# Buffers, feature sums and engine choices in a fused attention and gated-layer block on one core

## The chip, the cores and the metric

The kernel runs on one core of one Trainium2 chip. A core has five engines that work side by side and meet through semaphores: TensorE (PE in the profile, with its weight loads shown as PEld), VectorE (DVE), ScalarE (ACT), GpSimd (POOL) and SyncE (SP), which here only issues transfers. Matrix products land in PSUM, eight banks of 512 float32 numbers for each of 128 partitions; everything else lies in SBUF. The metric is device time in microseconds (us) of one execution, lower is better. The kernel before took 207.77 us (median of three runs, 207.37 to 208.1).

## The reference

The input x has 2048 rows of 448 bf16 numbers. Two blocks follow each other, each with a layer norm ahead of it and an addition of its own input behind it:

```python
def _A_ref(x, wqkv, w_phi, wo):                      # H = 16 heads, Dh = 28
    q, k, v = ...                                    # x @ wqkv, split by head
    pq = einsum("bhsd,hdf->bhsf", q, w_phi); pk = einsum("bhsd,hdf->bhsf", k, w_phi)
    phi_q = concat([softmax(pq), softmax(-pq)])      # over the 28 features of a head
    phi_k = concat([softmax(pk), softmax(-pk)])
    kv = einsum("bhsf,bhsd->bhfd", phi_k, v); z = einsum("bhsf->bhf", phi_k)
    num = einsum("bhqf,bhfd->bhqd", phi_q, kv)
    den = einsum("bhqf,bhf->bhq", phi_q, z)[..., None] + 1e-6
    return (num / den).reshape(B, S, D) @ wo

def _B_ref(x, w_gate, w_up, w_down):                 # F = 1792
    return (sigmoid(x @ w_gate) * (x @ w_up)) @ w_down

h  = x + _A_ref(layernorm(x), ...)
h2 = h + _B_ref(layernorm(h), ...)
```

So it is linear attention: a feature map of keys and values is summed over all rows (kv and z) before any query can be answered, and then a gated layer follows. The sum over all rows is the one place where everything has to come together.

## The kernel before

The 2048 rows are 16 tiles of 128 (t = 0 to 15); most later work goes by pairs of tiles (pr = 0 to 7), the queries by blocks of four tiles (c = 0 to 3), the gated layer by chunks of 2, 4, 4, 4 and 2 tiles.

Work is written as named tasks, each with the engines that may do it, the tasks it depends on and, for a PE task, the PSUM banks it may use. The order of all tasks is not computed at run time: the table `ORDER` (lines 40 to 88) lists one number for each task, 32 × (number of the task) + 4 × (choice of bank) + (choice of engine). `stored` reads it, and `emit` gives each engine its tasks in that order as a fixed instruction list, with a semaphore wait ahead of a task wherever something it needs is made by another engine. So each engine works strictly in order: if the task at the head of its list has to wait, all behind it wait.

The stages, by the names of the tasks:

- Loads. x comes in six transfers (x0 to x12 by first tile), the weights of attention in others, all ahead of the weights of the gated layer. `wqT`, `xT`, `oT` and `hT` are transposes done by transfers from SP's queue.
- First norm (lines 577 to 606). For each tile `bst` (statistics) and `agg` on VectorE; by batches of 1, 1, 2, 4, 4, 4 tiles `ve` and `rstd` (the power −0.5, on GpSimd), and for the later batches `mm` and `nm`, which make the negative mean times that power. `xn` writes the normalised tile to `xn_pad`, a ring of `NXP` tiles; tiles 0 to 3 are transposed on PE (`xP`, `xT`), the others by transfers.
- Keys and values (lines 626 to 700). `pa` and `pb` are the two parts of a tile's products with the folded key weights and the value weights, in two banks. `ekp` and `ekm` are the exponentials of both signs on ScalarE (`ek`, a ring of `NEK`), `v1` copies the values out. Then the softmax: `sa` and `ss` make the sums over the 28 features, `rs` the reciprocals, `phi` scales the exponentials (a ring of `NPHI`), and `kv` adds the tile's product of features and values in bank 4.
- In `sa` the two halves of the 28 features are added, 448 numbers from 896; `ss` then sums the rest with a reduce. A tile takes this way if it is in `SPLIT`, which holds all 16 tiles. `sa` writes `half_s`, a ring of `NSA` = 2.
- Queries (`qa`, `q`, `eqp`, `eqm`, lines 727 to 748), then `kvz`, which takes the summed features out of bank 4 once the last `kv` is done.
- Attention output (lines 758 to 895): `num` (products with `kvz`), `ocp` (copy to SBUF, ScalarE or VectorE), `rSm`, `rr`, `b`, `c`, `rd`, `o` on VectorE (the normalising factors and the output), `oT`, `woa` and `wo_` (product with wo), `h` or `hc` (addition of x), the second norm (`bst2`, `agg2`, `ve2`, `rstd2`, `hn`) and `hT`. Pair 0 is transposed on PE (`oP`, `hP`), the other pairs by transfers.
- Gated layer (lines 917 to 979): `ga` and `gu` are the two parts of gate and up for 128 of the 1792 columns, `sig` on ScalarE, `hh` on VectorE, `dn` the product with w_down, `fin` the last addition and `st` the store. It needs all its weights and the transposed tiles of its chunk.

In the order before, the scalings `phi` are all on VectorE; four of the sixteen `sa` are on VectorE (tiles 6, 10, 12, 15), twelve on GpSimd; `xn` of tiles 0 to 5, 8, 13, 14 on VectorE, the seven others on ScalarE; of the copies `ocp` tiles 1 and 3 on VectorE. The first products of features, `kv` of tiles 1 to 3, stand in PE's list ahead of the second part of tile 7, the one of tile 0 behind tile 2.

Of the kernel before, what the change touches and what calls it, by code (L numbers as in the profile page):

```python
# [5 lines left out]
dt = mybir.dt  # L6
# [34 lines left out]
544 576 0 480 1152 609 224 737 128 28416 160 640 96 28448 352 801 192 28480 768 256 448 28512 384 896 28544  # L41
992 28576 1952 832 28608 28640 960 1984 2017 2112 28672 2048 673 28704 2144 705 2080 28736 2336 2176 928 28768
2208 2272 864 1184 1088 2368 2304 1316 2240 1216 2720 1120 1384 1344 1260 288 2656 1409 4144 2400 1588 512
1281 4160 2432 1440 1636 2592 1600 4072 9632 1472 2464 1520 28800 2496 1665 28832 4096 4204 1537 2528 4276
4225 1056 2624 4576 2688 2560 4289 2752 2785 3104 2848 2816 4608 3168 10272 3040 4516 5824 1024 2881 5536 2913
4712 2945 5568 3136 3200 3072 4320 2976 4544 3232 5632 4736 3264 5792 3008 5664 5888 4640 5696 6304 4352 5601
320 4672 6368 3297 5728 6336 5856 1760 5920 3328 1700 6080 1832 3616 5760 1793 3744 3360 4772 6048 3392 6112
3425 3680 6144 1888 3456 4800 5952 1856 3776 3648 4384 6400 3552 4832 1728 6176 6560 4904 5984 6592 10304 3488
4864 6208 6656 10176 6432 4928 6624 10208 3712 3584 6464 6848 4964 3809 6240 6816 6496 3520 6016 6272 3873
6881 6912 6528 7072 4416 4992 7136 6688 3840 7104 5024 6944 7392 10240 6720 5096 1921 6976 9664 3904 7360 6752  # L50
5056 9696 7328 7169 5120 3936 7008 10408 7616 3969 7584 7200 7424 4448 6784 7840 7040 7232 7648 10432 7680
7456 7904 5216 7488 7872 7264 10464 5160 7520 4032 7712 7936 5248 5184 7744 10496 9728 7776 7296 7552 4001
8096 7808 8161 4480 8128 5284 7968 8384 8352 5352 8193 10336 8416 8448 8224 5312 10144 8000 5376 8256 416 8608
8032 10532 8640 8672 8705 8864 8064 8480 10560 8896 8288 8928 5476 9792 10592 8736 8960 9760 5416 8512 8544
10624 5504 8768 5440 8992 9376 8800 10788 9408 9152 9024 9473 9120 8320 8576 9056 9184 8832 10816 9440 9504
9216 10656 9536 10848 9248 11048 9568 10880 9280 10688 9312 9088 10720 9344 9824 9600 9856 11072 11424 10752
10368 11524 12524 11104 11553 11456 11488 12545 12452 12480 13216 11584 13292 11616 11136 11648 10916 12576
13312 11680 11176 12608 12640 9888 13248 14060 10944 11712 12672 14080 11200 11744 10976 12704 11904 13344
11864 12736 11804 11232 13376 12768 11873 12800 11808 11008 13408 11936 13440 11264 13996 14756 13472 11968
13504 14016 11304 13536 12032 13568 12096 14112 14828 14784 12064 11328 12128 14144 12160 12000 14176 12836  # L60
12192 14848 12224 14208 15584 12864 12288 15616 12256 12408 12896 12348 13600 12353 14240 12416 12928 15524
13632 15552 14272 17836 13664 11360 17856 18084 14880 17888 17952 12992 11392 18112 17920 17984 13696 18476
9920 18144 18016 13024 18600 12960 14304 13728 13056 14336 18048 18496 13088 18176 18624 13760 18528 18208
18656 18560 18340 18688 18240 13792 13152 16364 9952 18272 18728 13825 13120 16384 18368 18304 13856 13184
18752 14912 18400 18976 13920 18784 16300 18432 19008 13888 14372 18816 19040 13952 14944 16320 17064 14400
19072 14976 9984 19232 14432 18860 17088 19264 18880 16416 19492 18912 19368 18944 19520 15008 16448 19392
19552 20076 19424 19584 15648 20196 15040 15072 19456 15104 20096 14464 19944 15680 20128 10016 19296 20224
19328 10048 20160 19968 20256 20448 20000 20032 20588 20288 15144 16480 17124 15712 15168 10080 17152 20608
15200 10112 20480 20640 20708 20672 20512 15744 19112 19820 15232 16512 20736 20544 19136 15776 20768 19840
16544 19168 21344 19200 15808 20328 19872 20800 19904 21220 14528 20352 15296 20844 15264 16576 20384 14496  # L70
15328 20416 21248 15360 15392 14560 20864 21280 15840 15456 21480 15872 20896 21312 20928 21376 14593 20964
14624 21408 21100 14656 21440 20992 16608 15424 16640 17184 21120 21024 17216 14688 15904 17248 21152 15488
21056 21504 15936 14720 21536 19620 19712 19648 21184 21568 15968 21996 19744 22248 22496 22016 22528 22048
# [10 lines left out]
27200 25472 27552 26816 27584 28012 25504 26336 25536 27240 28032 26368 28064 27748 26400 27264 26432 27776  # L84
28096 27296 26848 27328 27372 26880 27808 27880 26912 27840 27392 26944 27620 27904 27424 27648 64 27456 26144
27680 27936 25964 26240 25984 26016 26048 26272 27968 26304 27712 26176 28136 26080 26112 19680 21952 23936
28224 24032 28160 21856 26208 28320 19776 28256 24128 28288 28192 28352 28384
"""


# [938 lines left out]
```

## Time and profile before

| | us |
|---|---|
| median of three runs | 207.77 |
| the profiled execution | 207.67 |
| its span, first to last instruction | 205.9 |
| PE busy | 197.2 |
| VectorE busy | 135.6 |
| ScalarE busy | 96.5 |
| GpSimd busy | 30.6 |

The page and its views name engines, lines and operations. A group reads: line, engine, operation, output and inputs, shapes, number of instructions, then busy time in us and mean length of one in ns, then the idle time of the engine ahead of them and what ended it. A stretch of the table of stretches has its two ends, its length, and for each engine the time it was busy in it. A timeline gives start, length and number of instructions of each piece. The chain that ended last is followed back from the last instruction, each step to what released it. [...]

The span is not the time of an execution: 1.8 us lie around it.

### The profile page before, as it was taken

What the parts mean: (1) busy time and instruction counts of PE and PEld (TensorE: products, weight loads), DVE (VectorE), ACT (ScalarE), POOL (GpSimd) and SP (SyncE); (2) the same over time, 40 slices, a digit from 0 to 9 for tenths busy, and PEclk for the clock granted to TensorE, in tenths of its full rate; (3) what the DMA queues carried; (4) which work ended last, traced back from release to release, by engine and by line L of the source; (5) the groups of instructions that cost most, each with busy time, mean ns of one, the idle gap of its engine ahead of it and who ended that gap; (6) DMA issues with size and microseconds to landing.
All of it is one profiled execution on the core that took longest, in us unless ns stands there. A gap on an engine that the chain in (4) does not pass through costs nothing.

```text
span 205.9 us, 5431 instructions
## 1 busy us (share of the span) xinstructions
PE 197.2 (96%) x2278; PEld 107.1 (52%) x2278; DVE 135.6 (66%) x312; ACT 96.5 (47%) x172; POOL 30.6 (15%) x56
## 2 busy tenths in 40 slices
PE   7899998998988999999999999999999999999993
PEld 2544555455445876554444444544444455796553
DVE  2999999997998996789823875435446415351241
ACT  2579999799998773443311333003334400442000
POOL 3738653420003110001100001100001000000000
PEclk9999999999999999999999999999999999999999
DMA  5996477764022493700450000620000031000034
GB/s 167 279 277 128 76 188 200 181 223 142 3 57 48 73 173 81 197 3 3 94 111 3 0 0 3 124 51 0 3 0 5 2 79 20 0 3 0 25 111 156
DMA packets 35109, 16.94 MB, mean 82 GB/s; under 512 B 26828, under 2 KB 34060, under 8 KB 35084
## 3 DMA queue, kind: packets, MB, share of 16 engines
q1 hardware_dynamic: 34140, 15.78, 33.1%
q10 hardware_dynamic: 944, 0.80, 1.4%
q8 instruction: 18, 0.29, 0.6%
q14 instruction: 7, 0.06, 0.1%
HBM read 8.98 MB, written 1.84 MB: 53 GB/s over the span
## 4 chain that ended last, share of the span: by engine, by line
PE 78%; DVE 12%; ACT 4%; DMA 2%; issue 1%; POOL 1%
PE bank L934 42%; PE bank L968 21%; PE bank L637 5%; PE bank L833 4%; PE bank L736 3%; DMA x_sb<-in_A_x_dram 2%; DVE phi L684 2%; PE bank L696 1%; DVE ssum L673 1%; DVE xn_pad L603 1%; DVE st L583 1%; ACT xn_pad L602 1%; ACT ek L659 1%; DVE b_sb L792 1%; DVE b_sb L795 1%
## 5 line engine op out<-in xcount | busy, mean ns | idle before, releaser
L934 PE MATMUL bank<-xnT,wg_sb 64*128 64x512 bf16 (+1 forms) x490 | 87.4, 333 | 0.1
L934 PE MATMUL bank<-xnT,wu_sb 64*128 64x512 bf16 (+1 forms) x490 | 87.4, 333 | 0.0
L943 ACT ACTIVATE sg_sb<-bank 128x512 f32<-128x512 f32 (+1 forms) x70 | 34.6, 513 | 77.9 <-PE bank L934 74.0
L951 DVE SCALAR_TENSOR_TENSOR hh<-sg_sb,bank 128x512 bf16<-128x512 f32 (+1 forms) x70 | 39.1, 576 | 28.4 <-ACT sg_sb L943 28.1
L934 PEld LDWEIGHTS bank<-xnT,wg_sb 64*128 64x128 bf16 x490 | 45.3, 94 | 21.9 <-issue 1.9
L934 PEld LDWEIGHTS bank<-xnT,wu_sb 64*128 64x128 bf16 x490 | 45.1, 94 | 15.5
L968 PE MATMUL bank<-wd_sb,hh 128*128 128x448 bf16 (+1 forms) x238 | 43.1, 342 | 0.0
L968 PEld LDWEIGHTS bank<-wd_sb,hh 128*128 128x128 bf16 x238 | 22.9, 98 | 20.1 <-issue 1.4
L975 DVE SCALAR_TENSOR_TENSOR x_sb<-bank,x_sb 128x448 bf16<-128x448 f32 (+1 forms) x17 | 9.9, 594 | 28.3 <-PE bank L968 28.3
L637 PE MATMUL bank<-Wk,xnT 64*128 64x448 bf16 x112 | 22.1, 350 | 0.4 <-ACT Wq L425 0.3
L637 PE MATMUL bank<-Wv,xnT 64*128 64x448 bf16 x112 | 21.6, 350 | 0.0
L746 ACT ACTIVATE eq<-bank 128x1024 bf16<-128x1024 f32 x16 | 16.3, 1067 | 0.7 <-PE bank L736 0.6
L871 POOL TENSOR_SCALAR rs<-mv 128x2 f32<-128x2 f32 x5 | 1.3, 256 | 99.6 <-DVE mv L869 50.3
L667 POOL TENSOR_TENSOR half_s<-ek 128x448 f32<-128x448 bf16 x12 | 12.9, 1078 | 15.3 <-ACT ek L657 7.0
L425 ACT CAST opm<-bank 128x960 bf16<-128x960 f32 x14 | 13.7, 1014 | 2.8 <-PE bank L772 2.1
L833 PE MATMUL bank<-wo_sb,oT 64*128 64x448 bf16 x112 | 13.3, 350 | 0.9 <-DVE oT L425 0.6
L736 PE MATMUL bank<-xnT,Wq 64*128 64x512 bf16 x112 | 14.0, 377 | 0.1
L637 PEld LDWEIGHTS bank<-Wk,xnT 64*128 64x128 bf16 x112 | 9.1, 94 | 6.9 <-PE bank L637 1.0
L637 PEld LDWEIGHTS bank<-Wv,xnT 64*128 64x128 bf16 x112 | 9.2, 94 | 4.3
L684 DVE TENSOR_TENSOR phi<-ek,rsum 128x896 bf16<-128x896 bf16 x16 | 10.3, 655 | 0.3 <-PE bank L696 0.2
L583 DVE BATCH_NORM_STATS2 st<-x_sb 128x6 f32<-128x448 bf16 x16 | 9.4, 612 | 1.7 <-DMA x_sb<-in_A_x_dram 1.7
L657 ACT ACTIVATE ek<-bank 128x448 bf16<-128x448 f32 x16 | 9.7, 630 | 1.3 <-PE bank L637 1.3
(91 smaller groups left out, 185.4 us busy)
## 6 DMA issues: line engine op xcount, KB each, us to landing
wg_sb<-in_B_w_gate_dram SPq DMA_DIRECT2D x4, 448.0 KB, 3.8
wu_sb<-in_B_w_up_dram SPq DMA_DIRECT2D x4, 448.0 KB, 3.7
out_dram<-x_sb SPq DMA_DIRECT2D x15, 112.0 KB, 1.8
wd_sb<-in_B_w_down_dram SPq DMA_DIRECT2D x7, 224.0 KB, 2.7
x_sb<-in_A_x_dram SPq DMA_DIRECT2D x2, 448.0 KB, 5.8
wq_raw<-in_A_wqkv_dram SPq DMA_DIRECT2D x4, 128.0 KB, 5.3
x_sb<-in_A_x_dram SPq DMA_DIRECT2D x2, 224.0 KB, 4.5
x_sb<-in_A_x_dram ACTq DMA_DIRECT2D x2, 224.0 KB, 4.9
```

The lines of the kernel that those rows point to most:

```text
L425: return e.copy(dst, src) if hasattr(e, "activation") else e.tensor_copy(dst, src)
L583: task(("bst", t), "dve", dve(D), lambda e, t=t: e.bn_stats(st1[:, t % 4, :], X(t)), [x_ld[t], opt(("agg", t - 4))])
L637: r = e.matmul(bank[bk][:, 0:D], lhsT=half(xnT, hi)[:, t, k, :], rhs=half(w, hi)[:, k, :], start=(i == 0), stop=(i == 6), tile_position=(6 ...
L667: task(("sa", t), None, 0.88, lambda e, t=t, s=s: e.tensor_tensor(half_s[:, t % NSA].rearrange("p (a n) -> p a n", a=4 * G), ek[:, s].rear ...
L684: task(("phi", t), None, 1.68, lambda e, t=t, s=s: e.tensor_tensor(phi[:, t % NPHI, :, :, 0:DH, :].rearrange("p a g d h -> p (a g) d h"), ...
L736: r = e.matmul(bank[bb[j]], lhsT=half(Wq2, hi)[:, k, 2 * g:2 * g + 2].rearrange("p c d h -> p (c d h)"), rhs=half(xnT, hi)[:, 4 * c:4 * c ...
L746: task((key, gp, c), "act", act_p(1024), lambda e, gp=gp, c=c, sg=sg, nm=nm: e.activation(eq[c][:, sg, 2 * gp:2 * gp + 2, :], wide[got(nm) ...
L833: r = e.matmul(bank[bb[j]][:, 0:D], lhsT=half(oT, hi)[:, pr % NO, j, k, :], rhs=half(wo_sb, hi)[:, k, :], start=(i == 0 and not res), stop ...
L934: r = e.matmul(bank[b][:, 0:N], lhsT=half(w, hi)[:, k, fs], rhs=half(hnT, hi)[:, t0:t0 + n, k, :], start=(i == 0), stop=(i == 6), tile_pos ...
L943: task(("sig", f_, c), "act", act_p(N), lambda e, j=j, N=N, nm=nm: e.activation(sg_sb[:, j % NSG, 0:N], bank[got(nm)[0]][:, 0:N], ACT.Tanh ...
L951: task(("hh", f_, c), "dve", dve(N), lambda e, j=j, N=N, nm=nm, f_=f_, c=c: e.scalar_tensor_tensor(hhT[c % 2][:, f_, 0:N], sg_sb[:, j % NS ...
L968: r = e.matmul(bank[b][:, c0:c1], lhsT=hhT[c % 2][:, f_, o:o + P], rhs=wd_sb[:, f_, c0:c1], start=(f_ == 0), stop=(f_ == FT - 1))
```

## The change

Five things are edited:

- Rings: `xn_pad` 8 to 10 tiles, `ek` 4 to 6, `phi` 3 to 6, `v1` 4 to 6, `opm` (the copied output products) 3 to 4.
- `SPLIT` is empty, so there is no `sa`, and `ss` of every tile is one reduce on VectorE over 896 numbers.
- `xn` of tiles 4 to 15 may also be done on GpSimd. (The test that picks the form of the instruction now asks for the task's engine.)
- `o` also waits for the two copies of pair 0's transposed output, which use the same ring.
- `ORDER` is another table, with other choices of engine and bank.

Decoded, the new table differs most in these places. `phi` of tiles 0, 1, 5, 7, 9, 10, 11 and 13 is on GpSimd. `xn` of tiles 5 to 11, 14 and 15 is on GpSimd, of 4 and 12 on ScalarE, of 13 and 0 to 3 on VectorE. Of the copies `v1`, tiles 0, 5 and 10 move from VectorE to ScalarE, 12 and 14 the other way. `ocp` of tile 7 moves to VectorE, one of pair 0's transposed copies from VectorE to ScalarE, and one the other way for the second norm. Of the variance steps `ve2`, five move from GpSimd to VectorE, one the other way. In PE's list the first value products stand ahead of the first key products, and `kv` of tiles 0, 1 and 2 stand together ahead of the second part of tile 7; `kv` of tiles 10 to 15 stand together behind the four query blocks that go ahead of them. On SP's queue the load of tiles 8 to 11 moves behind all loads of query and value weights, and the last two loads of the gate and up weights behind `oT` of pair 1.

```diff
@@ -38,53 +38,52 @@
 ORDER = """
-544 576 0 480 1152 609 224 737 128 28416 160 640 96 28448 352 801 192 28480 768 256 448 28512 384 896 28544
...
+544 737 0 480 1152 609 352 576 27904 128 288 640 27936 769 512 448 27968 800 224 256 28000 320 960 384 160 32
...
@@ -336,8 +335,8 @@
-    NXP, NEK, NPHI, NV, NOP, NO, NHP, NSG, NSA = 8, 4, 3, 4, 3, 2, 2, 4, 2
-    SPLIT = range(NT)
+    NXP, NEK, NPHI, NV, NOP, NO, NHP, NSG, NSA = 10, 6, 6, 6, 4, 2, 2, 4, 2
+    SPLIT = ()
@@ -386,7 +385,7 @@
-        half_s = sb("half_s", [P, NSA, D], dt.float32)
+        half_s = sb("half_s", [P, NSA, D], dt.float32) if len(SPLIT) else None
@@ -598,11 +597,11 @@
                     dst, src = xn_pad[:, s, :].rearrange("p (a n) -> p a n", a=2), lap(X(t))
-                    if hasattr(e, "activation"):
+                    if K.tasks[("xn", t)].eng == "act":
                         return e.activation(dst, src, ACT.Identity, bias=nm1[:, t:t + 1], scale=rs1[:, t:t + 1])
                     return e.tensor_scalar(dst, src, mv1[:, t, 0:1], rs1[:, t:t + 1], op0=ALU.subtract, op1=ALU.mult)
                 task(("xn", t), None, dve(160), f, [("rstd", a), opt(("nm", a)), free],
-                     engs=("dve",) if a < 4 else ("act", "dve"))
+                     engs=("dve",) if a < 4 else ("act", "dve", "pool"))
@@ -799,7 +798,7 @@
-                fac(rden[:, s2], DH), ALU.mult), [("rd", pr), opt(("oT", pr - NO))])
+                fac(rden[:, s2], DH), ALU.mult), [("rd", pr), opt(("oT", pr - NO)), opt(("oT", pr - NO, 0)), opt(("oT", pr - NO, 1))])
```

91 rows, old and new, of the table ORDER are left out of this document.

## The prediction

> **What bounds the kernel now.** I read four views in this order: the busy times of the page, the table of stretches, the chain that ended last, and then the groups and timelines of the stretch that the first three point at. The page's first part and the stretches (columns of a stretch: length, then busy time and instruction count of PE, PEld, DVE, ACT, POOL, then clock and DMA):
>
> ```profile
> PE 197.2 (96%) x2278; PEld 107.1 (52%) x2278; DVE 135.6 (66%) x312; ACT 96.5 (47%) x172; POOL 30.6 (15%) x56
> ```
> ```profile
> 4.40:16.00 11.60, 10.55 (x99) 5.68 (x97) 11.33 (x35) 7.32 (x16) 5.96 (x12) 1.00 1.17 272
> 16.00:49.40 33.40, 32.49 (x528) 16.95 (x528) 31.37 (x71) 31.38 (x60) 15.19 (x18) 1.00 0.68 175
> 49.40:67.10 17.70, 15.22 (x304) 8.19 (x304) 16.40 (x39) 16.81 (x22) 1.62 (x2) 1.00 0.16 31
> 67.10:202.70 135.60, 135.59 (x1344) 75.03 (x1344) 75.69 (x166) 39.73 (x77) 5.82 (x11) 1.00 0.22 48
> ```
>
> PE is busy 96% of the span, but the last row says where it can and cannot be helped: from 67.1 to 202.7 us it is idle 0.01 us, so nothing there can be gained. What the change can win lies ahead of 67 us, where PE, DVE and ACT are all nearly full. The chain tells which of them leads:
>
> ```profile
> 16.08 0.70 ACT xn_pad L602
> ...
> 18.08 0.42 ACT v L425
> 18.50 0.44 ACT ek L659
> ...
> 31.57 1.87 DVE phi L684 x2
> ...
> 47.76 0.88 PE bank L696 x48
> 48.64 0.75 PE bank L736 x6
> ...
> 62.01 0.52 POOL rs L871
> ...
> 62.61 1.11 POOL rs L873
> ...
> 63.75 0.42 DVE hn_pad L877
> ...
> 66.61 0.46 PE bank L934 x7
> ```
>
> Three stages: up to 48.64 us the keys' features (normalise, project, exponentials, sums, scaling, and their products on PE); up to 66.61 the attention output and the second norm of the first tiles; then the gated layer, PE alone. I call the end of the last feature product, 48.64 us, T. VectorE sets it. Its timeline holds the first sum, pairs that show the pace, the stalls and the last scaling:
>
> ```profile
> 7.79 1.03 DVE L603 TENSOR_SCALAR xn_pad<-x_sb,mv,rs 128x512 bf16<-128x512 bf16 x1
> ...
> 16.03 0.62 DVE L673 TENSOR_REDUCE ssum<-half_s 128x32 f32<-128x448 f32 x1
> ...
> 23.67 1.15 DVE L684 TENSOR_TENSOR phi<-ek,rsum 128x896 bf16<-128x896 bf16 x2
> ...
> 25.74 1.14 DVE L673 TENSOR_REDUCE ssum<-half_s 128x32 f32<-128x448 f32 x2
> ...
> 28.81 1.06 DVE L603 TENSOR_SCALAR xn_pad<-x_sb,mv,rs 128x512 bf16<-128x512 bf16 x1
> ...
> 31.57 1.87 DVE L684 TENSOR_TENSOR phi<-ek,rsum 128x896 bf16<-128x896 bf16 x2
> ...
> 47.18 0.62 DVE L684 TENSOR_TENSOR phi<-ek,rsum 128x896 bf16<-128x896 bf16 x1
> ```
>
> Two sums of 0.61 take 1.14 and two scalings of 0.62 take 1.15: the next instruction starts some 0.08 before the last ends, so a price on the path is the duration less 0.08. From 16.03 to 47.80 are 31.8 us. The groups, shapes kept apart (busy, mean ns):
>
> ```profile
> L684 DVE TENSOR_TENSOR phi<-ek,rsum 128x896 bf16<-128x896 bf16 x16 | 10.3, 655 | 0.3 <-PE bank L696 0.2
> L673 DVE TENSOR_REDUCE ssum<-half_s 128x32 f32<-128x448 f32 x16 | 9.6, 603 | 0.0
> L873 POOL TENSOR_TENSOR rs<-rs,neghalf 128x2 f32<-128x2 f32 x8 | 6.2, 770 | 5.8 <-DVE rs L871 5.4
> L682 DVE RECIPROCAL rsum<-ssum 128x32 bf16<-128x32 f32 x16 | 5.3, 339 | 0.2
> L588 POOL TENSOR_TENSOR rs<-rs,neghalf 128x4 f32<-128x4 f32 x3 | 3.3, 1115 | 0.3 <-DVE rs L586 0.3
> L425 DVE CAST opm<-bank 128x960 bf16<-128x960 f32 x2 | 2.2, 1152 | 0.5 <-PE bank L772 0.5
> L443 POOL TENSOR_SCALAR_AFFINE_SELECT ident<-ident 128x128 bf16<-128x128 bf16 x1 | 0.3, 292 | 0.0
> L450 DVE TENSOR_REDUCE dmask<-ident 128x2 f32<-128x112 bf16 x1 | 0.3, 270 | 1.5 <-POOL ident L443 1.5
> L436 POOL TENSOR_SCALAR_AFFINE_SELECT maskW<-maskW 112x4 f32<-112x4 f32 x1 | 0.2, 195 | 0.1
> ```
>
> My sum for VectorE in those 31.8 us: 16 sums at 0.53 = 8.5; 16 scalings at 0.54 = 8.6; 16 reciprocals at 0.26 = 4.2; 4 half sums at 0.54 = 2.2; 3 copies of v at 0.54 = 1.6; 4 statistics at 0.53 = 2.1; 3 normalisations at 0.33 = 1.0; small ones 0.6. That is 28.8. The two slow rows (1.06 against the usual 0.41, 1.87 against 1.15) add 0.65 and 0.72, and 1.6 are waits and gaps. VectorE is the bound of the stage, and the stalls are GpSimd's doing:
>
> ```profile
> 7.28 1.08 POOL L524 TENSOR_TENSOR Wp<-wphd,maskW 112x224 bf16<-112x224 bf16 x2
> ...
> 19.89 1.90 POOL L667 TENSOR_TENSOR half_s<-ek 128x448 f32<-128x448 bf16 x2 [0.44 <-ACT ek L657]
> ...
> 28.49 1.23 POOL L667 TENSOR_TENSOR half_s<-ek 128x448 f32<-128x448 bf16 x1 [1.52 <-ACT ek L657]
> ...
> 31.79 1.16 POOL L667 TENSOR_TENSOR half_s<-ek 128x448 f32<-128x448 bf16 x1 [0.28 <-ACT ek L659]
> ```
>
> The normalisation begun at 28.81 ends at 29.87, just after GpSimd's half sum (29.72); the second scaling of 31.57 ends at 33.44, after 32.95 plus its own half microsecond; the normalisation of 7.79 sits through both products of GpSimd, which end at 8.36.
>
> **The change, part by part.** The new table, decoded number by number (task, bank, engine), gives the order on each engine.
>
> Feature sums in one instruction. The half sums go: 4 on VectorE, 12 on GpSimd. Each of the 16 sums reads 896 numbers instead of 448. From 112 elements in 270 ns (same pattern, bf16) to 448 in 603 ns is 0.99 ns an element, so 448 more cost 0.45: 0.98 each, 15.7 in all, +7.2 on VectorE. I bound it by 0.9 and 1.1 each, that is 1.3 below and 1.9 above.
>
> Scalings on GpSimd. Tiles 0, 1, 5, 7, 9, 10, 11, 13: 8 × 0.54 = 4.3 off VectorE. On GpSimd a two-input instruction of 448 runs at 0.95 (two in 1.90), so 896 at about 1.85. It lies beside VectorE, except where GpSimd holds VectorE up, below. [...]
>
> Normalisations on GpSimd. Tiles 5 to 11, 14 and 15 go to GpSimd, 4 and 12 to ScalarE (0.70 each on its path, seven before), so ScalarE loses 3.5 us, and VectorE keeps one of the last twelve. The price on GpSimd is not in the trace: the one-input rows (4 elements 195 ns, 128 in 292) give 0.78 ns an element, 0.59 for 512; the two-input row gives 1.06. I take 0.65, near the one-input rows, since it reads one tensor; both ends stay for the range.
>
> More buffers. The rings of ek, phi and v go to six, of padded tiles to ten. PE and ScalarE may run six tiles ahead of the scaling instead of four or three, so a late scaling stops PE only where its product stands in PE's queue. They take no time.
>
> Where the stage begins. VectorE now has its first eight statistics, four normalisations and a dozen small ones done at about 11.8 (4.46 + 4.2 + 1.3 + 1.2 + 0.6 of waits). Then 1.05 on GpSimd for the power −0.5 of four variances (row of 1115), 0.2 for the mean; ScalarE does tile 4 (0.70), two copies of v (0.42) and four exponentials (0.44): the first sum starts at 16.6, against 16.03. The load of tiles 8 to 11 moves from seventh to eleventh on SP's queue:
>
> ```profile
> 8.02 0.47 SPq L461 DMA_DIRECT2D wq_raw<-in_A_wqkv_dram  x1
> ```
> ```profile
> wu_sb<-in_B_w_up_dram SPq DMA_DIRECT2D x4, 448.0 KB, 3.7
> ...
> x_sb<-in_A_x_dram SPq DMA_DIRECT2D x2, 448.0 KB, 5.8
> ```
>
> The eleventh was issued at 8.02; with 5.8 to landing it is there at 13.8, VectorE wants it at 12.4, and the statistics behind it (3.6) have until 16.6. So it costs between nothing and 0.8; I take 0.2. In exchange the two loads of v's weights go ahead, which only helps.
>
> The sum to T. VectorE from 16.8: 15.7 + 4.3 + 4.2 + two v copies 1.1 + two statistics 1.1 + one normalisation 0.3 + small ones 0.8 = 27.5, the same 1.6 of waits, and the time GpSimd holds it. Walking GpSimd's queue: three normalisations 13.2 to 15.2, power and mean to 17.0, three more to 18.9, scalings 1 and 0 from 19.1 to 22.8, tile 10 to 23.5. VectorE comes to its first scaling (tile 2) at 23.1: 0.4 lost. Tile 4's meets tiles 15 and 14 (0.15), tile 14's meets 13 and 11 (0.3). Together 0.85, against the 1.4 of before. 16.8 + 27.5 + 1.6 + 0.85 = 46.75, and 0.35 for the last product: T = 47.1, 1.55 earlier. PE needs 10.6 (eight pairs), 6.0 (four query blocks) and 3.9 (13 products) from about 25.4, thus 45.9: it just keeps up, so more than 2.7 cannot be won here.
>
> From T to the gated layer, 17.97 before. One copy of the output products (1152 ns, the row of L425) moves to VectorE ahead of the first transposed output, one transposed copy (0.33) leaves it: +0.8 on the path. Behind that, the variance step moves from GpSimd (0.52 at 62.01) to VectorE (about 0.16), and the power, 1.11 there against 770 ns in its group, no longer meets two-input work of VectorE: −0.7. Net +0.1. Bounds −0.4 and +1.0. The last two weight loads of the gated layer now stand behind the first output transpose on SP's queue, which waits for that output, about 55; issued at 56.5 with 3.7 to landing they are there near 60, 5 us ahead of their first use, so they cost nothing.
>
> From 66.61 on, all of PE's work stays; I cost the new order at nothing, with up to 0.5 for a stall, since VectorE and ScalarE have 60 and 96 us to spare there. The last store stays last.
>
> Sum: −1.55 + 0.1 = −1.45 from the profiled execution's 207.67 us (span 205.9; it stands 0.1 under the median of 207.77): 206.2 us.
>
> **The rivals.** *GpSimd becomes the bound (slower).* Place: the run of seven normalisations and two scalings on GpSimd ahead of VectorE's scaling of tile 2, and PE's first three products queued behind it. If a normalisation costs the two-input price 1.06, the run ends 2.3 later (six before the scalings and tile 10, less a pause of 0.5), VectorE is held until 25.8, and T is 49.4: 208.5 us; with scalings at 2.1 also, 209.0. It decides from about 0.9 per normalisation. For it: the row of 7.79, where VectorE was kept out through two instructions of GpSimd. Against: the one-input rows. [...]
>
> *The gain goes in the attention stage (no change).* ScalarE is busy 16.81 of 17.70 there; if its queue, and not the copy chain of VectorE, releases the first output, PE only waits longer for the same copies, and the +1.0 bound holds: 207.1 to 207.6 us. For it: the chain passes through copies of both engines there. Against: ScalarE enters the stage with the same eight exponentials behind it.
>
> *The change does not relieve VectorE.* 7.2 added, 4.3 + 2.2 + 1.0 and two statistics off: the net is 1.3 of 28.8. A sum at 1.1 instead of 0.98 eats it: 208.1, still within 0.3% of 207.77.
>
> **How the numbers follow.** The forecast, 206.2 with its own range 205.0 to 207.0, gets 0.56; GpSimd as the bound 0.26; the gain lost in attention, or to the dearer sum, 0.18. About 0.3%, 0.6 us, is what a measurement of this kernel can tell from no change, so faster 0.56, within it 0.18, slower 0.26. The range for 8 in 10 goes down to 204.9 (VectorE never held, sums at 0.9) and up to 208.8 (normalisations at the two-input price, and part of the dearer scalings).
>
> **What would show it.** Right: sums near 1.06 long, scalings on GpSimd 1.8 to 2.0 apart, normalisations there under 0.8, the last product near 47, the first gated matmul near 65.1, then PE without idle time to within 0.5. Wrong: VectorE's scaling of tile 2 over 1.5 long, PE waiting for phi between 22 and 26, T later than 48.6, or idle time of PE behind 67.

## The result and the profile after

The changed kernel takes 213.95 us (median of four runs, 213.12 to 214.65) against 207.72 (median of four runs of the kernel before): 1.0298 times the time before, 95% interval 1.0256 to 1.034. The forecast was 206.2 in a range up to 208.8. The profiled execution took 213.12, span 211.4. Here and below medians and ranges take in all runs, ratios and their intervals only runs within 1.5% of the fastest of their kernel.

First the busy times and the granted clock from its page:

```profile
PE 197.6 (93%) x2278; PEld 109.2 (52%) x2278; DVE 134.2 (63%) x300; ACT 94.3 (45%) x168; POOL 49.3 (23%) x56
...
PEclk9999966999999999999999999999999999999999
```

TensorE does the same work in a span longer by 5.5, so it waits more; VectorE has less to do than before, GpSimd 18.7 us more; and the clock falls in two of the 40 slices, where the profiled execution of the kernel before kept it full in all. The table of stretches, cut at the same three stages (columns as in the prediction):

```profile
16.00:55.20 39.20, 32.25 (x510) 17.27 (x512) 28.17 (x52) 27.96 (x53) 32.01 (x22) 0.91 0.56 125
55.20:72.70 17.50, 15.24 (x308) 8.45 (x308) 16.84 (x39) 16.99 (x22) 0.72 (x1) 1.00 0.39 85
72.70:208.50 135.80, 135.80 (x1354) 76.35 (x1348) 77.23 (x170) 39.09 (x77) 5.52 (x8) 1.00 0.20 48
```

The second and third stage are as long as before (17.50 against 17.70, 135.80 against 135.60). All of the loss lies in the key-feature stage. There VectorE, which led before (31.37 of 33.40), is busy 28.17 of 39.20, and GpSimd, busy 15.19 before, is busy 32.01, nearly as long as TensorE. The instruction that reads the summed features (`kvz`) starts when the last feature product ends, so it dates T; from the timelines of VectorE, before and after:

```profile
48.68 0.64 DVE L751 TENSOR_TENSOR kvz<-bank,dmask 128x464 bf16<-128x464 f32 x1 [0.88 <-PE bank L696]
```
```profile
54.46 0.64 DVE L750 TENSOR_TENSOR kvz<-bank,dmask 128x464 bf16<-128x464 f32 x1 [0.66 <-PE bank L695]
```

T went from 48.7 to 54.5, 5.8 later. The groups of the three edited operations (busy, mean ns):

```profile
L677 DVE TENSOR_REDUCE ssum<-ek 128x32 f32<-128x896 bf16 x16 | 16.7, 1069 | 3.9 <-ACT ek L658 2.2
L602 POOL TENSOR_SCALAR xn_pad<-x_sb,mv,rs 128x512 bf16<-128x512 bf16 x9 | 18.6, 2076 | 0.2
...
L683 POOL TENSOR_TENSOR phi<-ek,rsum 128x896 bf16<-128x896 bf16 x8 | 14.5, 1827 | 3.8 <-DVE rsum L681 2.8
```

These are lengths. The sums take 1.07, where the forecast named 1.06 (its 0.98 is the price on the path, 0.08 less), the scalings 1.83 (forecast 1.85), the normalisations 2.08 (forecast 0.65, bounds 0.59 to 1.06). GpSimd's timeline shows what that does to its queue, and one row of TensorE's what waits for it:

```profile
12.30 6.19 POOL L602 TENSOR_SCALAR xn_pad<-x_sb,mv,rs 128x512 bf16<-128x512 bf16 x3
...
20.14 6.21 POOL L602 TENSOR_SCALAR xn_pad<-x_sb,mv,rs 128x512 bf16<-128x512 bf16 x3
26.32 3.33 POOL L683 TENSOR_TENSOR phi<-ek,rsum 128x896 bf16<-128x896 bf16 x2
```
```profile
29.70 1.48 PE L695 MATMUL bank<-v,phi 128*64 128x58 bf16 x48 [4.86 <-POOL phi L683]
```

Six normalisations hold the queue for 12.4 us, so scalings 1 and 0 end at 29.65 where the forecast had 22.8. Three products of features stand at the head of TensorE's list; all that stands behind them, among it the projections that ScalarE and VectorE live on, waits 4.9 us with them. VectorE's own first scaling, of tile 2, is not held up (0.62), but soon VectorE too waits for GpSimd's list, for `nm` (minus mean times factor), which stands behind the two scalings:

```profile
23.77 0.62 DVE L683 TENSOR_TENSOR phi<-ek,rsum 128x896 bf16<-128x896 bf16 x1
...
33.03 0.41 DVE L602 TENSOR_SCALAR xn_pad<-x_sb,mv,rs 128x512 bf16<-128x512 bf16 x1 [6.50 <-POOL nm L592]
```

Then TensorE's clock is low:

```profile
25.00:30.00 5.00, 0.30 (x12) 0.31 (x14) 1.53 (x2) 0.26 (x1) 5.00 (x4) 0.81 0.39 73
30.00:35.00 5.00, 5.00 (x68) 2.71 (x64) 1.97 (x6) 3.69 (x8) 4.00 (x5) 0.51 0.92 232
```

At 0.51 TensorE's pairs of key and value products begin 0.37 apart (from 32.58 to 33.70), at 1.00 they begin 0.19 apart (from 22.97 to 23.54), so by an estimate the five microseconds do as much as 2.55 at full clock, and the second stretch loses 2.45; in the first, TensorE is idle anyway (0.30 busy). One more wait was not forecast. It is on the transposed query weights, here in the chain that ended last:

```profile
11.81 5.78 DMA WqT<-wq_raw
17.59 0.05 issue
17.63 0.37 PE bank L554 x4
```

### The profile page after: what moved, and what is told of

Same layout as the page of the kernel before. It is cut to its first block, busy times and chain, and to the rows that moved or that the text cites. A ratio compares the mean times of both kernels' runs of the same rounds, so it can differ in the third digit from the quotient of the medians.

```text
span 211.4 us, 5399 instructions
## 1 busy us (share of the span) xinstructions
PE 197.6 (93%) x2278; PEld 109.2 (52%) x2278; DVE 134.2 (63%) x300; ACT 94.3 (45%) x168; POOL 49.3 (23%) x56
## 4 chain that ended last, share of the span: by engine, by line
PE 81%; SPq 5%; POOL 4%; ACT 3%; DMA 3%; DVE 3%; issue 1%
PE bank L933 40%; PE bank L967 20%; PE bank L636 8%; PE bank L832 5%; SPq L460 4%; PE bank L735 3%; DMA WqT<-wq_raw 3%; ACT eq L745 2%; POOL xn_pad L602 2%; PE bank L695 2%; POOL phi L683 2%; PE bank L771 1%; SPq L500 1%; DVE o_pad L799 1%; DVE b_sb L791 1%
## 5 line engine op out<-in xcount | busy, mean ns | idle before, releaser
L636 PE MATMUL bank<-Wk,xnT 64*128 64x448 bf16 x112 | 23.6, 370 | 0.5 <-DMA xnT<-xn_pad 0.5
L636 PE MATMUL bank<-Wv,xnT 64*128 64x448 bf16 x112 | 23.7, 370 | 0.0
L872 POOL TENSOR_TENSOR rs<-rs,neghalf 128x2 f32<-128x2 f32 x8 | 6.0, 760 | 63.3 <-DVE rs L870 63.2
L677 DVE TENSOR_REDUCE ssum<-ek 128x32 f32<-128x896 bf16 x16 | 16.7, 1069 | 3.9 <-ACT ek L658 2.2
L602 POOL TENSOR_SCALAR xn_pad<-x_sb,mv,rs 128x512 bf16<-128x512 bf16 x9 | 18.6, 2076 | 0.2
L683 POOL TENSOR_TENSOR phi<-ek,rsum 128x896 bf16<-128x896 bf16 x8 | 14.5, 1827 | 3.8 <-DVE rsum L681 2.8
L735 PE MATMUL bank<-xnT,Wq 64*128 64x512 bf16 x112 | 14.1, 377 | 0.5 <-DVE opm L424 0.5
L424 ACT CAST opm<-bank 128x960 bf16<-128x960 f32 x13 | 12.5, 974 | 1.7 <-PE bank L771 1.7
L636 PEld LDWEIGHTS bank<-Wk,xnT 64*128 64x128 bf16 x112 | 9.7, 99 | 6.6 <-DMA xnT<-xn_pad 0.9
L636 PEld LDWEIGHTS bank<-Wv,xnT 64*128 64x128 bf16 x112 | 9.7, 99 | 5.7 <-issue 1.8
L656 ACT ACTIVATE ek<-bank 128x448 bf16<-128x448 f32 x16 | 8.9, 559 | 6.6 <-POOL phi L683 4.8
```

The costliest lines, as they stand in the source:

```text
L424: return e.copy(dst, src) if hasattr(e, "activation") else e.tensor_copy(dst, src)
L602: return e.tensor_scalar(dst, src, mv1[:, t, 0:1], rs1[:, t:t + 1], op0=ALU.subtract, op1=ALU.mult)
L636: r = e.matmul(bank[bk][:, 0:D], lhsT=half(xnT, hi)[:, t, k, :], rhs=half(w, hi)[:, k, :], start=(i == 0), stop=(i == 6), tile_position=(6 ...
L677: task(("ss", t), "dve", dve(896), lambda e, s=s: e.tensor_reduce(ssum[:, s, :].rearrange("p (a h) -> p a h", h=2), ek[:, s].rearrange("p ...
L683: task(("phi", t), None, 1.68, lambda e, t=t, s=s: e.tensor_tensor(phi[:, t % NPHI, :, :, 0:DH, :].rearrange("p a g d h -> p (a g) d h"), ...
L735: r = e.matmul(bank[bb[j]], lhsT=half(Wq2, hi)[:, k, 2 * g:2 * g + 2].rearrange("p c d h -> p (c d h)"), rhs=half(xnT, hi)[:, 4 * c:4 * c ...
```

## The experiments

The theory from these rows, N: a normalisation on GpSimd takes 2.08, and the six in front of the first scalings make the loss. Rivals: S, the scalings on GpSimd and their hold on VectorE; R, something in the order or the rings. In the diffs below "order" means numbers of the table that name another engine or another place. Times of the kernel before beside them are medians on the same chip.

**Normalisations back.** From the changed kernel:

```diff
 order: xn of tiles 5 to 11, 14, 15
-  on GpSimd
+  on the engine each had before (VectorE or ScalarE);
+  tile 4 goes back from ScalarE to VectorE too
```

> The changed kernel with one thing undone: the nine normalisations on GpSimd go back to the engines they had before (tiles 6, 7, 9, 10, 11, 12, 15 on ScalarE, 4, 5, 8, 13, 14 on VectorE), at the same places of the order. Theory N (2.08 us for a normalisation on GpSimd, six of them ahead of scalings 1 and 0, is what costs): the run on GpSimd shrinks by 6 x 2.08 = 12.5, scalings 1 and 0 end near 22 instead of 29.7, PE does not stop for 5 us and keeps its clock; 205.5 to 207.5. [...] Rival R (one sum of 896 is too dear for VectorE): 210 or more.

Measured: 207.52 us (207.1 to 210.99, 10 runs), ratio 1.0024 (0.9999 to 1.0049). T, by the same row of VectorE's timeline:

```profile
48.24 0.64 DVE L750 TENSOR_TENSOR kvz<-bank,dmask 128x464 bf16<-128x464 f32 x1 [0.66 <-PE bank L695]
```

The nine normalisations alone carry the whole loss, and S and R fall as its cause. Sums in one instruction, scalings on GpSimd, rings and order together come out even.

**Scalings back.**

```diff
 order: phi of tiles 0, 1, 5, 7, 9, 10, 11, 13
-  on GpSimd
+  on VectorE
```

> The changed kernel with the eight scalings of GpSimd put back on VectorE, the nine normalisations left on GpSimd (and the wait of a normalisation for the transpose that reads its ring slot written out, which is met long before). Theory N: tile 8's transpose still waits for the third normalisation of the second run (26.4) and lands near 29.6, where tile 8's products need it, so PE stops at nearly the same time for some 4 us: 210 to 214. Rival S: the stall goes with the scalings, 206 to 208.5.

(In this kernel and in the later ones with three late normalisations or with earlier query weights, a normalisation also waits for the transpose that reads its place in the ring.) Measured: 213.32 us (211.38 to 214.34), ratio 1.0277 (1.0211 to 1.0342), T at 52.7. Without any scaling on GpSimd most of the loss stays; what is late then are the normalised tiles themselves. Timelines of GpSimd and of TensorE:

```profile
20.02 8.24 POOL L602 TENSOR_SCALAR xn_pad<-x_sb,mv,rs 128x512 bf16<-128x512 bf16 x4
```
```profile
29.39 0.36 PE L638 MATMUL bank<-Wk,xnT 64*128 64x448 bf16 x1 [2.85 <-DMA xnT<-xn_pad]
```

**TensorE kept busy ahead of the late product.**

```diff
+ 21 matmuls on constant data, into a bank not in use,
+ ahead of the product of features of tile 0
```

> The changed kernel with 21 matmuls of 512 columns on constants added ahead of the first feature product, where PE is idle from 24.6 to 29.7; they write a free bank and nothing reads them. If the granted clock of 0.51 from about 30 to 35 us comes from the idle time, it stays at 1.00, the fourteen pairs of products run 0.19 instead of 0.37 apart, and the time falls by 1.9 to about 212.0; the 5 us of waiting stay. If the clock has another cause, no change: 213.9.

Measured: 213.62 us (212.13 to 216.34), ratio 1.0278 (1.0233 to 1.0323). From 25 to 35 us the clock was now 1.00, but in the profiled execution it fell at other places, 0.74 from 20 to 25 and 0.85 from 60 to 65; the one run at a mean clock of 0.999 took 212.13, and T in the profiled execution was 53.3. By that one run the clock costs about two of the six microseconds; in the others the place where it falls was moved, the loss was not removed.

**Sums in one instruction alone,** in the kernel before:

```diff
-    SPLIT = range(NT)
+    SPLIT = ()
 order: the 16 half sums left out, nothing else
```

> The kernel before with one part of the change alone: no half sums, one sum of 896 on VectorE for each tile; rings, engines and order as before. By the ledger of VectorE (16 x 0.46 more, 4 half sums of 0.54 less: +5.2 of work where it is the bound, of which its 1.6 of waits can take a part) the last feature product comes 3.5 to 5 later: 211 to 213. If VectorE is not the bound of that stage, 207.5 to 208.5.

Measured: 209.64 us (209.56 to 209.72), ratio 1.011 (1.0091 to 1.013), T 2.0 later (50.71). The edit costs by itself, less than expected. With GpSimd's half sums the stalls on VectorE go too: the pair of scalings behind the normalisation of tile 13, 1.87 before, takes 1.09, and that normalisation 0.41 in place of 1.06. The 5.2 of added work less the 1.4 of stalls and the 1.6 of waits are 2.2, and VectorE has no wait left in the stage.

```profile
30.09 0.41 DVE L602 TENSOR_SCALAR xn_pad<-x_sb,mv,rs 128x512 bf16<-128x512 bf16 x1
...
33.13 1.09 DVE L683 TENSOR_TENSOR phi<-ek,rsum 128x896 bf16<-128x896 bf16 x2
```

That the scalings on GpSimd pay for it in the changed kernel is the ledger of the prediction; no run has these two parts alone.

**What makes a normalisation slow.** Nine normalisations on GpSimd in one program, six of them in other forms, five of which compute something else than the normalised tile:

```diff
+ tile 7:  x * factor + constant          tile 6:  (x + constant) * constant
+ tile 11: copy                           tile 9:  as it was, but 512 elements in a row
+ tile 8:  product with the factor spread out as a tensor
+ tile 10: product of two tensors         tiles 5, 15, 14: as they were
```

> The kernel after, with seven of its nine GpSimd normalisations changed in form and the first and the last two left as they were; what those seven compute is another function of x, so the output is another. The question is what makes one take 2.07 us where the forecast had 0.65. Theory 'operand': the two scalars that come from memory per partition make it slow; then the form with two constants takes 1.1 us or less, the one with one scalar from memory lies between, and the contiguous one stays at 2.07. Theory 'view': the overlapping source view of twice 256 elements makes it slow; then the contiguous one takes 1.1 or less and all others that read through the view stay near 2.07. Theory 'engine': any tensor_scalar of 512 elements takes about 2.07 here; then these three forms are alike within 10%, and only the copy and the products of two tensors differ (the products by the feature rows 1.83 us for 896, so about 1.05).

GpSimd's timeline in order, tiles 5, 7, 6, 11, 9, 8, 10:

```profile
12.60 2.08 POOL L618 TENSOR_SCALAR xn_pad<-x_sb,mv,rs 128x512 bf16<-128x512 bf16 x1
14.67 0.69 POOL L604 TENSOR_SCALAR xn_pad<-x_sb,rs 128x512 bf16<-128x512 bf16 x1
15.44 0.62 POOL L606 TENSOR_SCALAR xn_pad<-x_sb 128x512 bf16<-128x512 bf16 x1
...
17.55 0.61 POOL L608 COPY xn_pad<-x_sb 128x512 bf16<-128x512 bf16 x1
18.15 2.08 POOL L610 TENSOR_SCALAR xn_pad<-x_sb,mv,rs 128x512 bf16<-128x512 bf16 x1
20.20 1.04 POOL L613 TENSOR_TENSOR xn_pad<-x_sb,rs 128x512 bf16<-128x512 bf16 x1
...
24.48 1.54 POOL L615 TENSOR_TENSOR xn_pad<-x_sb 128x512 bf16<-128x512 bf16 x1
```

'View' falls (2.08 with and without it), 'engine' falls (0.62 to 0.69 for other forms). I read it as 'operand': two scalars from memory cost, one does not. That reading was wrong, as the split into two instructions shows below; none of the fast forms here has a subtract. The single execution took 206.92 us.

**Three late normalisations left on GpSimd.**

```diff
 order: xn of tiles 5, 6, 7, 8, 9, 11
-  on GpSimd, ahead of the scalings of tiles 1 and 0
+  on the engine each had before (and tile 4 on VectorE); tiles 10, 14, 15 stay on GpSimd
```

> The kernel after with only the normalisations of tiles 10, 14 and 15 left on GpSimd; the six that stood ahead of the scalings of tiles 1 and 0 go back to the engines of before. If the loss came from the place, six normalisations in front of the first two scalings, then three of the same 2.07 us in GpSimd's later holes cost nothing: the state's end at 47.7 to 48.7, 206.8 to 207.9 us in all, GpSimd busy 6.2 us longer than without them. [...]

Measured: 207.53 us (205.8 to 208.04, 12 runs), ratio 0.9969 (0.994 to 0.9999); T at 47.5, 0.75 earlier than with none on GpSimd. Three instructions of 2.1 us in holes of the queue cost nothing here; the place decides whether the price counts. The runs fall in two groups: five at a clock of 0.998 or more take 205.8 to 206.2, seven at 0.992 take 207.5 to 208.0.

**Query weights transposed earlier,** with all normalisations off GpSimd, and the same edit with the three late ones on it:

```diff
 SP's queue
-  wo 5, wo 7, x 12, wqT 1, wqT 0
+  wqT 1, x 12, wqT 0, wo 5, wo 7
```

> The kernel with all normalisations off GpSimd, and on SP's queue the two transposes of the query weights moved ahead of two loads of output weights (one of them also ahead of the load of x tiles 12 to 15). If the wait of 1.8 us on these transposes is what ate the forecast gain, it shrinks to below 0.5 us and the time falls to 205.8 to 206.8 us. Rival: ScalarE's own run of work sets the pace up to 19.8 us (the chain of waits runs through it there), so PE's wait is hidden by it: it shrinks and the time stays at 207.2 to 207.8.

> Both edits of the two kernels beside it: three normalisations on GpSimd in its holes (which takes two off ScalarE) and the transposes of the query weights earlier. If waits on the weights and on ScalarE each hide the other, only both together give time: 205.3 to 206.5 us. If VectorE sets the stage's pace, 16 sums at 1.07 and what else it has, neither matters and it stays at 207.0 to 207.8.

Measured: 210.29 us (210.12 to 210.42, 4 runs), ratio 1.0128 (1.0093 to 1.0162), and 206.85 (205.84 to 208.92, 12 runs), ratio 0.9969 (0.9934 to 1.0005). The transposes are issued earlier, but TensorE's wait does not shrink, so neither run tests what the wait is worth. SP's queue and TensorE's wait, first with the order of the change (normalisations back), then with the transposes first:

```profile
10.09 4.00 SPq L500 DMA_TRANSPOSE WqT<-wq_raw  x2
```
```profile
17.58 0.37 PE L554 MATMUL bank<-Wp,WqT 112*128 112x112 bf16 x4 [1.62 <-DMA WqT<-wq_raw]
```
```profile
8.92 1.35 SPq L500 DMA_TRANSPOSE WqT<-wq_raw  x1
...
11.01 1.24 SPq L500 DMA_TRANSPOSE WqT<-wq_raw  x1
```
```profile
17.94 0.37 PE L554 MATMUL bank<-Wp,WqT 112*128 112x112 bf16 x4 [1.75 <-DMA WqT<-wq_raw]
```

The last issue ends at 12.25 and not at 14.1, and the data are there no earlier, so something behind the issue sets the landing; the DMA share of the stretch from 15 to 20 us, 1.02 and 1.09, points to the transfers themselves, which is not shown. With three late normalisations T is 47.5 with the edit and without it. All four runs of the first of the two stood at a clock of 0.981 to 0.984, by that figure 3 to 4 us of their time (an estimate), and T came at 50.0; why its clock fell in every run is open.

**The forecast's price given to the instruction.** From the changed kernel, the mean not taken off, so that part of the computation is missing:

```diff
-  (x - mean) * factor
+  x * factor + 0.0                       (the nine on GpSimd)
```

> The kernel after with the nine GpSimd normalisations reduced to one scalar from memory: x times the row's factor, without the mean taken off, so the output lacks that part. One then takes about 0.69 us, the price that the forecast had. If the price of this instruction was the only step that failed, the forecast of the rest comes out: key-feature stage ended at 47 to 48.2 us, 206.0 to 207.0 us in all. If something else that came with the change (its order, longer rings, sums in one instruction) costs as well, it stays above 208.

Measured: 206.91 us (205.0 to 210.61, 10 runs), ratio 0.9947 (0.9921 to 0.9973). With a normalisation of 0.69 the loss is gone, and the median is 0.7 above the forecast's 206.2, with a wide spread of runs. T was 48.6 in the profiled execution, 0.4 later than expected; that one stood at a clock of 0.984, with 0.84 and 0.82 in the stretches from 15 to 25 us.

**Two instructions for one,** to test the reading 'two scalars cost':

```diff
-  (x - mean) * factor
+  y = (x - mean) + 0.0
+  y * factor + 0.0
```

> The kernel after, where each GpSimd normalisation is written as two instructions, mean off and then times the factor, each with one scalar from memory. If the second scalar from memory is what costs, the two together take 1.4 to 1.6 us against 2.07, GpSimd's run up to the first scaling shortens by 3 to 4 us, TensorE's gap ahead of the first feature products falls from 5.1 to 1 to 2 us, and the time to 208 to 210 us. If GpSimd pays by the element for each pass over data that others use as well, two passes cost no less than one: 213 or more.

Measured: 217.05 us (216.81 to 217.56), ratio 1.0464 (1.0447 to 1.0482): slower than the change itself. GpSimd's timeline, three of the first step and three of the second:

```profile
12.68 5.96 POOL L608 TENSOR_SCALAR xn_pad<-x_sb,mv 128x512 bf16<-128x512 bf16 x3
18.62 2.03 POOL L605 TENSOR_SCALAR xn_pad<-xn_pad,rs 128x512 bf16<-128x512 bf16 x3
```

Taking off one scalar takes 1.99, multiplying by one 0.69. It is not the number of scalars.

**Longer rings alone,** in the kernel before (`opm` stays at 3):

```diff
-    NXP, NEK, NPHI, NV, NOP = 8, 4, 3, 4, 3
+    NXP, NEK, NPHI, NV, NOP = 10, 6, 6, 6, 3
```

> The kernel before with longer rings alone (10 normalised tiles, 6 exponentials, 6 feature tiles, 6 value tiles), its order as it was. Waits on a free buffer were not in the rows, so no change: 207.2 to 207.8 us. If the longer rings let work run ahead by themselves, 206.8 or less; if they cost (more of SBUF touched, other waits), 208 or more.

Measured: 207.32 us (206.83 to 209.01, 10 runs) against 207.57, ratio 0.9988 (0.9966 to 1.001): nothing, as forecast.

**TensorE kept busy through two waits,** on the kernel with three late normalisations on GpSimd:

```diff
+ 7 matmuls on constant data ahead of the first product on the query weights
+ 6 ahead of the transposes of the first attention output
```

> The kernel with three normalisations on GpSimd, and 13 matmuls without use where TensorE waits (7 ahead of the first product on the query weights, 6 ahead of the first output transposes), which keep it busy through two of its waits of 1.6 us. If a stretch of idle TensorE is what lowers the clock in those runs that take 207.5 to 208.0, they go, and all runs stand at 205.7 to 206.4, 0.993 to 0.995 of the kernel before. If the clock falls for another reason, both kinds of run remain; if the dummies are in the way of the products behind them, 206.5 or more.

Measured: 206.55 us (206.26 to 206.88), ratio 0.995 (0.9936 to 0.9963). The runs at a lower clock are gone (0.999 to 1.000 in all five); the dummies cost about 0.6 against the runs at full clock without them (205.8 to 206.2), and T comes 0.7 later, at 48.2.

**Subtract, scalars, or the mean.** Again nine in one program, seven of them computing something else:

```diff
+ tile 7:  (x - constant) * constant      tile 6:  (x + mean) * constant
+ tile 11: (x + mean) * factor            tile 9:  x * factor - mean
+ tile 8:  x * factor + third scalar      tile 10: difference of two tensors
+ tile 15: (x - factor) + constant        tiles 5, 14: as they were
```

> The kernel after, with seven of its nine GpSimd normalisations changed in form, in the order in which they run: as it was; subtract a constant, times a constant; add the mean, times a constant; add the mean, times the factor; times the factor, subtract the mean; times the factor, add a third scalar from memory; difference of two tensors; subtract the factor, add a constant; as it was. What they compute is another function of x, so the output is another. Theory 'subtract': every one-tensor form with subtract takes 1.9 to 2.1 us, every one with add and multiply alone 0.6 to 0.8, with one scalar from memory or two. Theory 'two scalars': the three forms with two scalars from memory take about 2.07, those with one 0.7, whatever the operation. Theory 'where the mean lies': forms that read the mean take 2.0, those that read other scalars 0.7.

In the order 5, 7, 6, 11, 9, 8, 10, 15:

```profile
12.38 2.08 POOL L617 TENSOR_SCALAR xn_pad<-x_sb,mv,rs 128x512 bf16<-128x512 bf16 x1
14.54 1.92 POOL L602 TENSOR_SCALAR xn_pad<-x_sb 128x512 bf16<-128x512 bf16 x1
16.45 0.69 POOL L604 TENSOR_SCALAR xn_pad<-x_sb,mv 128x512 bf16<-128x512 bf16 x1
...
18.67 0.77 POOL L606 TENSOR_SCALAR xn_pad<-x_sb,mv,rs 128x512 bf16<-128x512 bf16 x1
19.43 2.08 POOL L608 TENSOR_SCALAR xn_pad<-x_sb,rs,mv 128x512 bf16<-128x512 bf16 x1
21.49 0.77 POOL L610 TENSOR_SCALAR xn_pad<-x_sb,rs,nm 128x512 bf16<-128x512 bf16 x1
...
25.51 1.54 POOL L612 TENSOR_TENSOR xn_pad<-x_sb 128x512 bf16<-128x512 bf16 x1
...
31.93 2.00 POOL L614 TENSOR_SCALAR xn_pad<-x_sb,rs 128x512 bf16<-128x512 bf16 x1
```

'Subtract' meets all seven rows with one tensor, the other two theories fail: a subtract by a constant takes 1.92, an addition of the mean with the factor behind it, two scalars from memory, 0.77. A second scalar adds 0.08. The difference of two tensors (1.54) costs what their product costs (1.54 above), so it is this instruction with this operation, not subtraction as such.

**The same normalisation without subtract.** The program already holds minus mean times factor for ScalarE:

```diff
-  e.tensor_scalar(dst, src, mv1[:, t, 0:1], rs1[:, t:t + 1], op0=ALU.subtract, op1=ALU.mult)
+  e.tensor_scalar(dst, src, rs1[:, t:t + 1], nm1[:, t:t + 1], op0=ALU.mult, op1=ALU.add)   (GpSimd's nine)
```

> The kernel after with its nine GpSimd normalisations written as x times the factor plus (minus mean times factor), which the program holds already for ScalarE: two scalars from memory, no subtract, the same output. If subtract is what costs, one takes 0.65 to 0.8 us, GpSimd is busy 37 us and not 49, the key-feature stage ends at 47 to 48 us and the time is 205.0 to 207.0. If two scalars from memory cost, it stays at 212 to 214.5.

> The kernel beside it with 13 matmuls without use, 7 ahead of the first product on the query weights and 6 ahead of the first output transposes. If idle TensorE is what lowers the clock in some runs, its runs stay at a clock of 0.999 or 1.000 and within 1 us of each other, at 205.3 to 206.5, while those of the kernel beside it spread by 2 us or more. If not, both spread alike.

Measured: 206.28 us (204.81 to 208.01, 12 runs) against 207.81, ratio 0.9914 (0.9879 to 0.9948); with the 13 dummy matmuls 206.14 (205.39 to 207.16, 6 runs), ratio 0.9919 (0.9889 to 0.9949). Both beat the kernel before and the changed one. The group of the normalisation and the row that dates T, of the first of the two:

```profile
L603 POOL TENSOR_SCALAR xn_pad<-x_sb,rs,nm 128x512 bf16<-128x512 bf16 x9 | 6.8, 767 | 0.2
```
```profile
46.91 0.64 DVE L752 TENSOR_TENSOR kvz<-bank,dmask 128x464 bf16<-128x464 f32 x1 [0.66 <-PE bank L697]
```

T at 46.9 where the change had 54.5: one operation in nine instructions is worth 7.6 us there. Of its twelve runs six at a clock of 0.999 or more take 204.8 to 205.5, and six at 0.992 take 207.1 to 208.0. So the median of 206.28 lies in a gap where no run is. The dummies hold all six runs of the other at 1.000, though these still spread over 1.8 us, more than expected, for a reason that is open; their median is no better.

## Why the prediction was wrong

**The step that failed** is the price in "Normalisations on GpSimd": "I take 0.65, near the one-input rows, since it reads one tensor; both ends stay for the range." It measured 2.08, twice the upper end of 1.06 (the row of 0.95 for 448 elements scales to 1.09, which would have changed nothing). For other operations the price was nearly right: a copy, an addition or a product of one tensor takes 0.61 to 0.77 for 512 elements. But the rows that it came from held no subtract, and I bounded by the number of inputs when the operation decided. No row could have warned me, since the trace of before has no tensor_scalar with subtract on GpSimd; the range should have been open upward there. The forms of tensor_scalar without subtract took 0.62 to 0.77 here, the forms with it 1.92 and more.

**The rest of the sum nearly held.** With the form without subtract in place T is 46.9, where 47.1 was forecast. That is two small errors of opposite sign: the first sum starts at 15.95 and not at 16.8, and from there to the end of the last scaling are 30.3 us and not 29.95. The sums (1.07 long, 1.06 forecast) and the scalings are as priced, and the rings by themselves cost nothing. From T to the first gated matmul (72.71 in the chain of the changed kernel) are 18.3 against 17.97, +0.3 where +0.1 was said in bounds of −0.4 to +1.0. ScalarE's exponentials of the queries now stand in the chain there (3.77 from 52.17), the place that the second rival named; with them the stage is 0.3 longer and no more. The variance step and the power took 0.16 and 0.72 there (68.39 and 68.64 in the changed kernel) against 0.51 and 1.10 before, as forecast; but that power ran beside a two-input addition of VectorE (1.09 from 68.50), so that such work is what lengthens it is not shown. Behind it TensorE is busy all the time; the rest takes 138.7 against 139.3, where the forecast had no gain. That the time came out at 206.28 where 206.2 was said is luck: the six runs at the full clock that the forecast assumed take 204.8 to 205.5, about 1.1 us less, and the six others 207.1 to 208.0.

**The rival had the right place and a price too low.** "GpSimd becomes the bound" named the run of normalisations ahead of the first scalings, TensorE's three products behind it, and "about 0.9" as the point where it decides. The sign it gave, TensorE waiting for phi between 22 and 26, came, from 24.8 to 29.7. Its other sign did not: VectorE's scaling of tile 2, which it had over 1.5 long, took 0.62. The hold on VectorE, for which it quoted the row of 7.79, was not what cost; VectorE waited 6.5 us for `nm` from GpSimd's list instead. Its own two points, 47.1 at 0.65 and 49.4 at 1.06, are a slope of 5.6 us of T for 1 us of price; at 2.08 they give 55.1, and 54.5 was measured. That is in part luck, since the rival had no loss of clock in it, and the low clock behind the wait is in the 54.5. Its 208.5 was low because its price was. The scalings at 2.1 behind its 209.0 and in the upper end of the range stand in no run; they took 1.83.

**Two things were not in the prediction.** One is TensorE's wait of 1.7 on the query weights. In the kernel before TensorE came to these products at 17.8 and found the weights there; now it comes at 16.0, with one of the products moved ahead of the second part of tile 2, and waits for them to land at 17.6. Whether the wait moves T is not shown. The dummies fill it and do not shorten it, and the earlier transposes did not shorten it either. Rows of the kernel with product and addition suggest that it does: the exponentials of tile 2 stand behind it in ScalarE's list, and VectorE waits for them:

```profile
17.89 0.37 PE L554 MATMUL bank<-Wp,WqT 112*128 112x112 bf16 x4 [1.86 <-DMA WqT<-wq_raw]
```
```profile
21.60 2.08 DVE L679 TENSOR_REDUCE ssum<-ek 128x32 f32<-128x896 bf16 x2 [1.85 <-ACT ek L658]
```

The other is the clock, which I took for 1.00 throughout. It is part of the six microseconds (about two, by the one run with 21 dummies that had almost none of it), and in the repaired kernel it decides between about 205.1 and 207.4, nearly as much as the 2.7 that the runs at full clock win over the kernel before.

## What to carry to other kernels

A price for an operation that the trace does not hold is not bounded by rows of other operations on the same engine, even with the same shape and inputs (here 0.61 to 0.77 us without subtract, 2.08 with it); if one unknown price stands several times in front of a wait, measure it by itself first, or write the step in a form whose price is known (here a product and an addition in place of subtract and product). Before an instruction is moved to a slow queue, count what stands behind it there: three normalisations of 2.1 us in holes of GpSimd's queue cost nothing, six in front of the first scalings cost six microseconds. And a variant with the disputed instruction left out or cheapened tells in one run whether anything else is wrong.

## What the runs showed of the hardware

- On GpSimd tensor_scalar over 512 bf16 elements takes 0.62 to 0.77 us with add and multiply and, in the run of the other operations, 1.92 to 2.14 with subtract in either place, with constants or scalars from memory. Why is not shown.
- TensorE's clock fell after waits of 1.35 and 1.86 us (to 0.73 and to 0.82 in a stretch of 5 us), and not in every run. The stretches behind the wait on the query weights, of the kernel with the factor alone and then of the one with product and addition, where it began at about 16.0 and lasted 1.86 us in both:

```profile
15.00:20.00 5.00, 3.14 (x29) 1.47 (x26) 4.58 (x9) 2.84 (x8) 4.38 (x6) 0.84 1.09 161
20.00:25.00 5.00, 5.00 (x50) 2.56 (x49) 2.71 (x7) 3.78 (x9) 2.56 (x3) 0.82 0.48 96
```
```profile
15.00:20.00 5.00, 3.14 (x40) 1.60 (x38) 4.50 (x9) 3.48 (x9) 4.82 (x6) 1.00 1.04 161
20.00:25.00 5.00, 5.00 (x82) 2.71 (x80) 3.40 (x10) 4.70 (x12) 2.70 (x4) 1.00 0.75 175
...
55.00:60.00 5.00, 4.35 (x42) 1.90 (x44) 4.24 (x9) 3.87 (x5) 0.00 (x0) 0.73 0.72 227
```

With the same wait the clock is 0.82 in one execution and 1.00 in the other, which in turn loses it behind a wait of 1.35 that ends at 55.44. That idle TensorE is the cause is shown by the dummies (eleven runs of two kernels at 0.999 or more, against seven of twelve and six of twelve at 0.992 without them); what decides in a single run, and how long a wait has to be, is not.
